# Keys and queries laid out features by rows, values by token, cum sent straight to rows, and product times in the planner: a fused attention and two-layer kernel

## Chip, cores and metric

One core of one Trainium2 chip. The metric is the device time of one execution in microseconds (us); three runs of the kernel before gave 899.12, 900.30 and 899.88, so a median of 899.88.

## What is computed

```python
def _attn_ref(q, k, v, f):               # 4 x 8 heads x 576 tokens x 64
    scores = scale * np.matmul(q, k.transpose(0, 1, 3, 2))
    cum = np.cumsum(np.log(np.clip(f, 0.0001, 1.0)), axis=-1)
    decay = cum[:, :, :, None] - cum[:, :, None, :]
    scores = np.where(causal, -1000000000.0, scores + decay)
    scores = scores - np.max(scores, axis=-1, keepdims=True)
    attn = np.exp(scores)
    attn = attn / (np.sum(attn, axis=-1, keepdims=True) + 1e-09)
    return np.matmul(attn, v)

def _moe_ref(x, w_in, w_out, g_ln):      # 2304 x 512, inner 1024
    h = x @ w_in
    e = np.exp(h - np.max(h, axis=-1, keepdims=True))
    solu = h * (e / (np.sum(e, axis=-1, keepdims=True) + 1e-09))
    mu, var = mean(solu), mean((solu - mu) ** 2)
    return ((solu - mu) / np.sqrt(var + 1e-06) * g_ln) @ w_out

def _moe2_ref(x, w_in, w_out):           # inner 2048
    h = np.maximum(x @ w_in, 0.0)
    return h * h @ w_out
```

The second layer takes the first's output, and the first takes the attention's. The weights come as 64-bit floats. Every large product is made of rounded single-precision parts: a number is split into a high part (rounded to the type of a fast product) and a low part (the rest), and three products (low x high, high x low, high x high) are added.

## The kernel before

The work is written as a list of steps. Each has the engines that it may run on with a duration that the planner assumes, a priority (a due time in ns), and what it reads and writes. `Plan.lay` simulates the engines with these durations: on each engine it takes, among the steps that could start first, the one of the smallest priority, and where a step may run on several engines, the one that is free first (VectorE only if it would end 650 ns sooner than the others). What comes out is the order of instructions on each engine (PE is TensorE, DVE VectorE, ACT ScalarE, POOL GpSimd); all DMAs stand in one order on SP's queue. On the chip the engines then run in that order and wait for each other by semaphores. So the assumed durations and the due times set the order, and nothing else.

**Attention** runs over 20 tiles of queries (five per sequence, four of 128 tokens and one of 64; the short one is last in sequences 0 and 2, first in 1 and 3), and in each tile over 8 heads. `load` (line 348) fetches keys, queries and values of a tile, 256 KB each in runs of 256 bytes, tokens by rows. `prep_k` (396) and `prep_q` (431) transpose them on TensorE, four products per tile and tensor (`transposed`, 366, line 372), into one of three PSUM buffers that other work uses as well. From there two copies make the high parts, two VectorE instructions (420 for keys, 443 for queries) the low parts, and `dup` (383, line 389) copies the high parts to the other 64 rows on GpSimd or by a DMA. A product has 128 rows: K1 and Q1 hold the high part on 64 rows and, on two of the others, the cumulated log decay (cum) in two parts against ones; K2 and Q2 hold low and high parts. So two products per head (479) give the scores with the decay of the keys. The masking and the row minimum run on VectorE (499), the exponential on ScalarE (513), the normalization on GpSimd (540), the transposes of the weights on TensorE (556) with a copy out of PSUM (278), and the products with the values on TensorE (577, `mix`).

**cum** is made at the start: f is loaded, clipped (1116), its logarithm taken (1119), summed by a scan over 576 columns (1127), split in two parts (1130, 1133), stored to DRAM (1104) and read back from there to the rows of K1 (412).

**First layer.** `weights1` converts its weights from 64 bits to a high and a low part (`convert`, 598: lines 618, 622, 626, 632, 636 and copies on 278 to 284). `first` (740) multiplies (761 to 763), takes the exponential and the layer norm, and `out1` (689) multiplies by the second weight (702 to 704), as soon as 128 tokens of attention are there.

**Second layer.** Its weights are converted (`weights2`) into the room that attention leaves, and `step` multiplies six blocks of 384 tokens (1033 to 1035, 1063 to 1065).

Due times come from `att_ns` (322, what a head should take on TensorE), `EACH` (the first layer's share), at least MINSLOT = 1150 ns per head, from T0 on.

## Time and profile before

| | us |
|---|---|
| median of three runs | 899.88 (899.12 to 900.30) |
| the profiled execution: its own time | 900.41 |
| its span, first to last instruction | 898.4 |
| TensorE busy in the span | 850.7 (95%) |
| VectorE, ScalarE, GpSimd busy | 504.8, 477.8, 322.9 |
| mean granted clock of TensorE, share of 2.4 GHz | 0.994 |
| moved by DMA | 65.27 MB in 99264 packets, 65440 under 512 bytes |

Busy time is a share of the span and says nothing of a stage. A table of stretches shows the same by stage. The chain of waits is followed back from the last instruction: a piece's time there is elapsed time, while the durations of TensorE's instructions overlap. In lists of waits the engine that waits stands first, then what it waited for.

### The profile page before, as it was taken

Reading aid. Unit: us, or ns where it says so; the run is one execution under the profiler, and the core shown is the slowest. Engines: PE = TensorE matmul, PEld = TensorE weight load, DVE = VectorE, ACT = ScalarE, POOL = GpSimd, SP = SyncE. Lnnn points to the kernel's source line nnn. Section 1 sums busy time; section 2 is a strip of 40 time slices with the busy share of each in tenths; the row PEclk is TensorE's granted clock in tenths of the full one; section 3 lists DMA queues with packets and bytes.
Section 4 is the critical chain, followed back from the end, with each engine's and each line's share of the span. In section 5 each row is a group of like instructions: output and inputs, shape, how many; then the busy total and the mean of one; then the engine's idle time right before and its main releaser. Section 6 shows DMA issues by size and latency. Waiting matters only on the chain.

```text
span 898.4 us, 15951 instructions
## 1 busy us (share of the span) xinstructions
PE 850.7 (95%) x5440; PEld 734.1 (82%) x5440; DVE 504.8 (56%) x1463; ACT 477.8 (53%) x1242; POOL 322.9 (36%) x503
## 2 busy tenths in 40 slices
PE   4898999999999999999989687999999999999998
PEld 3666788888888888888879676899899999999997
DVE  8998777765776667765599889222222222222221
ACT  6789766677666667765667666223322322322222
POOL 7988843333333344432588778100000000000000
PEclk9899999999999999999999999999999999999999
DMA  8644331122411224010546643005002002000000
GB/s 220 161 107 124 94 87 36 49 66 57 88 42 43 59 62 97 26 48 25 185 130 200 200 131 115 1 1 175 36 1 71 36 1 72 36 1 1 35 1 36
DMA packets 99345, 66.29 MB, mean 74 GB/s; under 512 B 65440, under 2 KB 89248, under 8 KB 99264
## 3 DMA queue, kind: packets, MB, share of 16 engines
q1 hardware_dynamic: 99264, 65.27, 25.6%
q8 instruction: 43, 0.70, 0.3%
q14 instruction: 38, 0.31, 0.1%
HBM read 49.51 MB, written 14.30 MB: 71 GB/s over the span
## 4 chain that ended last, share of the span: by engine, by line
PE 77%; DVE 12%; ACT 3%; issue 3%; POOL 3%; DMA 1%; SPq 0%; POOLq 0%; ACTq 0%; DVEq 0%
PE pp L1033 6%; PE pp L1034 6%; PE pp L1035 6%; PE z L479 6%; PE xo L577 6%; PE pp L556 6%; PE pp L702 3%; PE hp L761 3%; PE hp L762 3%; PE hp L763 3%; PE pp L703 3%; PE pp L704 3%; PE hp L1063 2%; PE hp L1064 2%; PE z L1065 2%
## 5 line engine op out<-in xcount | busy, mean ns | idle before, releaser
L1044 DVE CAST q<-q 128x384 fp32r<-128x384 f32 x96 | 40.5, 422 | 252.6 <-PE pp L1065 92.2
L1041 ACT ACTIVATE q<-pp 128x384 f32<-128x384 f32 x96 | 47.0, 490 | 232.5 <-PE pp L1035 230.5
L540 POOL TENSOR_SCALAR adj<-adj,st 128x128 f32<-128x128 f32 (+9 forms) x160 | 92.0, 577 | 172.7 <-DVE st L536 75.8
L513 ACT ACTIVATE adj<-z,st 64x288 f32<-64x288 f32 (+9 forms) x192 | 95.7, 501 | 33.9 <-DVE st L499 19.5
L479 PE MATMUL z<-k,q 128*128 128x256 f32 (+8 forms) x384 | 96.2, 344 | 6.2 <-ACT adj L513 6.0
L278 ACT COPY pt<-pp 128x256 f32<-128x256 f32 (+5 forms) x170 | 69.0, 423 | 46.3 <-PE pp L556 43.6
L702 PE MATMUL pp<-ln,woh 128*128 128x256 f32 x288 | 84.5, 293 | 0.4 <-POOL woh L282 0.4
L556 PE MATMUL pp<-ident,adj 128*128 128x128 f32 (+1 forms) x480 | 77.8, 275 | 6.0 <-POOL adj L540 2.6
L703 PE MATMUL pp<-ln,wol 128*128 128x256 f32 x288 | 81.2, 282 | 0.1
L499 DVE CUSTOM_DVE_ANT_0 z<-z,maskb 128x128 f32<-128x128 f32 (+8 forms) x144 | 65.9, 460 | 27.4 <-PE z L479 25.6
L704 PE MATMUL pp<-ln,woh 128*128 128x256 f32 x288 | 81.1, 281 | 0.0
L556 PEld LDWEIGHTS pp<-ident,adj 128*128 128x128 f32 (+1 forms) x480 | 53.1, 141 | 26.5 <-POOL adj L540 10.3
L479 PEld LDWEIGHTS z<-k,q 128*128 128x128 f32 (+1 forms) x384 | 57.5, 185 | 16.1 <-ACT adj L513 10.2
L577 PE MATMUL xo<-pt,vn 128*64 128x128 f32 (+1 forms) x960 | 68.1, 274 | 0.1
L577 PEld LDWEIGHTS xo<-pt,vn 128*64 128x64 f32 x960 | 49.5, 138 | 20.0 <-issue 13.5
L761 PE MATMUL hp<-wih,xl 128*128 128x512 f32 x144 | 61.8, 429 | 0.5 <-ACT hp L800 0.5
L763 PE MATMUL hp<-wih,xh 128*128 128x512 f32 x144 | 57.2, 397 | 0.0
L762 PE MATMUL hp<-wil,xh 128*128 128x512 f32 x144 | 57.1, 397 | 0.0
L702 PEld LDWEIGHTS pp<-ln,woh 128*128 128x128 f32 x288 | 54.4, 189 | 2.8 <-issue 1.0
L703 PEld LDWEIGHTS pp<-ln,wol 128*128 128x128 f32 x288 | 54.4, 189 | 0.7 <-DVE wol L636 0.3
L704 PEld LDWEIGHTS pp<-ln,woh 128*128 128x128 f32 x288 | 54.3, 189 | 0.0
L1043 ACT ACTIVATE q<-q 128x384 f32<-128x384 f32 x96 | 50.3, 524 | 2.4
(481 smaller groups left out, 2260.7 us busy)
## 6 DMA issues: line engine op xcount, KB each, us to landing
x2d<-xc SPq DMA_DIRECT2D x72, 128.0 KB
pt<-in_moe_w_in_dram SPq DMA_DIRECT2D x22, 256.0 KB
pt<-in_moe_w_out_dram SPq DMA_DIRECT2D x22, 256.0 KB
vn<-in_v_dram SPq DMA_DIRECT2D x20, 256.0 KB
ln<-x2d SPq DMA_DIRECT2D x24, 192.0 KB
out_dram<-pt SPq DMA_DIRECT2D x18, 256.0 KB
kn<-in_k_dram SPq DMA_DIRECT2D x16, 256.0 KB
qn<-in_q_dram SPq DMA_DIRECT2D x16, 256.0 KB
```

The source lines that it names most:

```text
L278: nc.scalar.copy(dst(), src())
L479: nc.tensor.matmul(dst, lhsT=ql[:, p, 0:m], rhs=rhs, start=(g == 0), stop=(g == 1))
L513: nc.scalar.activation(out=adj[0:m, c[1] : c[2]], in_=Z[c[0]][0:m, 0 : c[2] - c[1]], func=AF.Exp, bias=st[0:m, low : low + 1], scale=-1.0, ...
L540: nc.gpsimd.tensor_scalar(out=adj[0:m, 0:ext], in0=adj[0:m, 0:ext], scalar1=st[0:m, 5:6], scalar2=1.0, op0=ALU.mult, op1=ALU.mult,)
L556: nc.tensor.transpose(at(sk)[:, (c - g) * m : (c - g + 1) * m], adj[0:m, zc : zc + P], ident[0:m, 0:m])
L577: nc.tensor.matmul(XO[own[j], p, off : off + m], lhsT=VN[vslot[b, c]][:, (2 * p + j) * D : (2 * p + j + 1) * D], rhs=pts[j][:, c * m : (c ...
L702: nc.tensor.matmul(px, lhsT=woh[:, fc, w], rhs=lo, start=(fc == 0), stop=False)
L703: nc.tensor.matmul(px, lhsT=wol[:, fc, w], rhs=hi, start=False, stop=False)
L704: nc.tensor.matmul(px, lhsT=woh[:, fc, w], rhs=hi, start=False, stop=(fc == KF - 1))
L761: nc.tensor.matmul(HP[:, c], lhsT=XL[i][:, cc, :], rhs=wih[:, cc, w], start=(cc == 0), stop=False)
L762: nc.tensor.matmul(HP[:, c], lhsT=XH[i][:, cc, :], rhs=wil[:, cc, w], start=False, stop=False)
L763: nc.tensor.matmul(HP[:, c], lhsT=XH[i][:, cc, :], rhs=wih[:, cc, w], start=False, stop=(cc == KC - 1))
```

## The change

Keys and queries are laid out on the host: per tile and half of the heads (0 to 3, 4 to 7) the 64 features stand on 64 rows, and once more on the other 64, with heads and tokens along the row. So a tile is loaded in two DMAs per tensor (256 KB each for 128 tokens) in runs of 2 KB, and no transpose is needed. KN and QN hold the two halves of one tile, where they held two tiles. Values come by token with all heads in a row.

`prep_k` copies 128 rows (K1 then holds the high part twice) and makes the low part on VectorE or GpSimd from the loaded tile and K1; `prep_q` copies the high part twice (to Q2 and to the other rows of Q1) and makes the low part on VectorE. `dup` and `fill` are gone. cum stands on 16 rows of K2 (8 heads, two parts), the same for every head, and Q2 has ones on the two rows of its head (`picks`, from the identity). The second product of the scores has 80 rows. Heads are numbered by half: `j, p = divmod(h, 4)`.

At the start clip, logarithm and scan are cut into columns 0 to 127 and the rest; the parts of the first 128 columns go by DMA from SBUF to K2, and the way over DRAM serves the later tiles.

The planner's times for products are changed, with them the due times, and T0 is 10000 for 16000.

```diff
+    AUX = slice(D, D + 2 * H)
+    HH = H // 2
...
+    K1 = [new(f"k1{j}", [HH, KW], F32R) for j in range(2)]
+    K2 = [new(f"k2{j}", [HH, KW], F32R) for j in range(2)]
+    Q1 = [[new(f"q1{i}{j}", [HH, P], F32R) for j in range(2)] for i in range(2)]
+    Q2 = [[new(f"q2{i}{j}", [HH, P], F32R) for j in range(2)] for i in range(2)]
...
     def att_ns(T):
         t, m = T["t"], T["m"]
-        return 2 * max(107, T["ext"] / 2.4) + 53 + (t + 1) * m * (109 + 135) / 128 + 109
-    EACH = 24 * 216 + 48 * 109 + 872
+        return 2 * max(118, 0.4375 * T["ext"] + 6) + (t + 1) * 109 * (m / 128 + 1) + 130
+    EACH = 24 * 231 + 48 * 119 + 872
...
-    def load(n, prio):
+    def load(nm, dst, src, n, prio):
         T = tiles[n]
...
+        m, o = T["m"], HH * T["q0"]
+        for j in range(2):
+            pl.add(
+                dict(dma=800 * m / P),
+                lambda j=j: nc.sync.dma_start(dst[j][:, 0 : HH * m], src[T["b"], j, :, o : o + HH * m]), prio + 2 * j,
+                writes=[(nm, j)],
+            )
+    def load_k(n, prio):
+        load("kn", KN, k, n, prio)
+    def load_q(n, prio):
+        load("qn", QN, q, n, prio + 1)
+    def load_v(n, prio):
+        b, t = tiles[n]["b"], tiles[n]["t"]
+        vslot[b, t] = n % NV
         def fn():
...
+            nc.sync.dma_start(VN[n % NV], v[b, t * P : t * P + P])
+        pl.add(dict(dma=800), fn, max(prio + 4, V0), writes=[("vn", n % NV)])
+    def picks(i, j):
         def fn():
...
+            c = D + HH * j
+            a, b = (ident[AUX, x : x + HH].unsqueeze(2).broadcast_to([2 * H, HH, P]) for x in (c, c + H))
+            eng = nc.gpsimd if s.on == "pool" else nc.vector
+            eng.tensor_tensor(out=Q2[i][j][AUX], in0=a, in1=b, op=ALU.add)
+        s = pl.add(dict(dve=602, pool=1252), fn, -6.9e6 if i == 0 else 5000, ["ident"], [("qa", i, j)])
     def prep_k(n, prio):
         T = tiles[n]
         m, b, q0 = T["m"], T["b"], T["q0"]
         kc = kcol(b, T["t"])
         cs = slice(kc, kc + m)
-        fresh = b == 0 or (b == 1 and T["t"] < 2)
-        sk, tp = transposed(KN[n % 2], m, prio, [("kn", n % 2)])
+        los = {}
         for j in range(2):
...
+            raw = KN[j][:, 0 : HH * m].rearrange("p (h s) -> p h s", s=m)
+            hk, lk = kcells("kh", j, kc, kc + m), kcells("kl", j, kc, kc + m)
+            def lo(j=j, raw=raw):
+                eng = nc.gpsimd if los[j].on == "pool" else nc.vector
+                eng.tensor_tensor(out=K2[j][LO, :, cs], in0=raw[LO], in1=K1[j][LO, :, cs].bitcast(F32), op=ALU.subtract)
+            def auxrows(y, j=j):
+                if n:
+                    src = cumd[y, b, :, q0 : q0 + m]
+                else:
+                    src = XH[0][0:H, y, :].bitcast(F32)
+                dst = K2[j][D + y * H : D + y * H + H, :, cs].bitcast(F32)
+                nc.sync.dma_start(dst, src.unsqueeze(1).broadcast_to([H, HH, m]))
+            copy(HH * m, lambda j=j: K1[j][:, :, cs], lambda raw=raw: raw, prio + 2 * j, [("kn", j)], hk, psum=False)
+            los[j] = pl.add(
+                dict(dve=67 + 1.045 * HH * m, pool=119 + 2.213 * HH * m), lo, prio + 2 * j, [("kn", j)] + hk, lk
+            )
+            for y in range(2):
+                rk = [f"cumd{y}"] if n else [("c0", 0), ("xh", 0, 0)][y : y + 1]
+                pl.add(
+                    dict(dma=350), lambda y=y, auxrows=auxrows: auxrows(y), prio + 2 * j, rk,
+                    writes=kcells(f"ka{y}", j, kc, kc + m),
                 )
...
     def prep_q(n, prio):
         m = tiles[n]["m"]
         i = n % 2
-        q1, q2 = Q1[i], Q2[i]
-        sk, tp = transposed(QN[i], m, prio, [("qn", i)])
         for j in range(2):
...
+            q1, q2 = Q1[i][j], Q2[i][j]
+            raw = QN[j][:, 0 : HH * m].rearrange("p (h s) -> p h s", s=m)
+            for rows, dst, nm in ((LO, q2, "qh"), (HI, q1, "qd")):
+                copy(
+                    HH * m, lambda rows=rows, dst=dst: dst[rows, :, 0:m], lambda rows=rows, raw=raw: raw[rows],
+                    prio + 2 * j, [("qn", j)], [(nm, i, j)], (), SC, False,
+                )
+            def lo(q1=q1, q2=q2, raw=raw):
                 nc.vector.scalar_tensor_tensor(
-                    out=q2[j][other[j], :, 0:m], in0=tp()[own[j]], scalar=SC,
-                    in1=q1[j][own[j], :, 0:m].bitcast(F32), op0=ALU.mult, op1=ALU.subtract,
+                    out=q1[LO, :, 0:m], in0=raw[LO], scalar=SC, in1=q2[LO, :, 0:m].bitcast(F32), op0=ALU.mult,
+                    op1=ALU.subtract,
                 )
...
+            pl.add(dict(dve=67 + 1.045 * HH * m), lo, prio + 2 * j, [("qn", j), ("qh", i, j)], [("ql", i, j)])
...
-            for g, (ql, kr) in enumerate(((Q1[i][j], K1[j]), (Q2[i][j], K2[j]))):
-                rhs = kr[:, p, k0 + a : k0 + e]
+            for g, (ql, kr, r) in enumerate(((Q1[i][j], K1[j], P), (Q2[i][j], K2[j], AUX.stop))):
+                rhs = kr[0:r, p, k0 + a : k0 + e]
                 dst = z[0:m, 0 : rep * (e - a)]
                 if rep > 1:
-                    rhs = rhs.unsqueeze(1).broadcast_to([P, rep, ext])
+                    rhs = rhs.unsqueeze(1).broadcast_to([r, rep, ext])
                     dst = dst.rearrange("p (r x) -> p r x", x=ext)
...
+                nc.tensor.matmul(dst, lhsT=ql[0:r, p, 0:m], rhs=rhs, start=(g == 0), stop=(g == 1))
+        rk = [(c, i, j) for c in ("qh", "ql", "qd", "qa")]
+        for c in ("ka0", "ka1", "kh", "kl"):
             rk += kcells(c, j, k0, k0 + ext)
         for c, k_ in zip(cuts, zk):
-            mm = max(107, (c[2] - c[1]) / 2.4 + 2.5)
+            mm = 0.4375 * rep * (c[2] - c[1]) + 6
...
-        pl.add(dict(pe=(t + 1) * 270 * m / P), fn, prio, rk, ["xo"])
+        pl.add(dict(pe=(t + 1) * 218 * m / P + 200), fn, prio, rk, ["xo"])
...
-                pl.add(dict(pe=654), fn, prio, rk, [sk], take=sk if g == 0 else None, uses=[sk] if g else [])
+                pl.add(dict(pe=714), fn, prio, rk, [sk], take=sk if g == 0 else None, uses=[sk] if g else [])
...
-                    dict(pe=648), fn, a + d * FH * (c * KC + cc) / 8, xk + [("wi", cc, c, y) for y in "hl"], ["h"]
+                    dict(pe=693), fn, a + d * FH * (c * KC + cc) / 8, xk + [("wi", cc, c, y) for y in "hl"], ["h"]
...
-                dict(pe=6 * 162.5), up, prio, rk, [ck], take=ck if cc0 == 0 else None, uses=[ck] if cc0 else []
+                dict(pe=6 * 174), up, prio, rk, [ck], take=ck if cc0 == 0 else None, uses=[ck] if cc0 else []
...
+    load_k(0, -8e6)
+    load_q(0, -8e6)
+    load_v(0, -8e6)
+    ones = E[0 : B * H, P : P + S]
     pl.add(dict(dve=20), lambda: nc.vector.memset(mhalf, -0.5), -9.1e6, [], ["mhalf"])
+    pl.add(dict(pool=460), lambda: nc.gpsimd.memset(ones, 1.0), -9.1e6, [], ["ones"])
+    pl.add(dict(pool=700), lambda: make_identity(nc, ident), -8.9e6, [], ["ident"])
     pl.add(
         dict(act=1283 + 94), lambda: nc.scalar.activation(out=ST[1][:, 0:1], in_=mhalf, func=AF.Ln, scale=-1.0), -9.1e6,
         ["mhalf"], [("st", 1, 0)],
     )
...
+    c0 = [XH[0][0 : B * H, a, :] for a in range(2)]
+    for y, (a, e) in enumerate(((0, P), (P, S))):
+        w = slice(a, e)
+        n = e - a
+        def scan(w=w, a=a):
+            nc.vector.tensor_tensor_scan(
+                out=cu[:, w], data0=ones[:, w], data1=lf[:, w], initial=cu[:, a - 1 : a] if a else 0.0, op0=ALU.mult,
+                op1=ALU.add,
+            )
+        pl.add(
+            dict(dve=68 + 0.522 * n),
+            lambda w=w: nc.vector.tensor_scalar(
+                out=fl[:, w], in0=fl[:, w], scalar1=1e-4, scalar2=1.0, op0=ALU.max, op1=ALU.min
+            ), -9e6 + y, ["f"], [("f", y)],
+        )
+        pl.add(
+            dict(act=94 + 0.833 * n), lambda w=w: nc.scalar.activation(out=lf[:, w], in_=fl[:, w], func=AF.Ln),
+            -9e6 + y, [("f", y)], [("lf", y)],
+        )
+        pl.add(
+            dict(dve=200 + 2 * n), scan, -9e6 + y, [("lf", y), "ones"] + ["cu0", ("xh", 0, 0)] * y, [f"cu{y}"]
+        )
+        if y == 0:
+            pl.add(dict(dve=135), lambda: nc.vector.tensor_copy(c0[0], cu[:, 0:P]), -9e6, ["cu0"], [("c0", 0)])
+            pl.add(
+                dict(dve=201),
+                lambda: nc.vector.tensor_tensor(out=c0[1], in0=cu[:, 0:P], in1=c0[0].bitcast(F32), op=ALU.subtract),
+                -9e6, ["cu0", ("c0", 0)], [("xh", 0, 0), ("xh", 0, 64)],
+            )
     pl.add(
         dict(act=1283 + 94), lambda: nc.scalar.activation(out=ST[0][:, 0:1], in_=mhalf, func=AF.Exp), -9e6,
-        ["mhalf", ("adj", 1, 0), ("adj", 1, 1)], [("st", 0, 0)],
+        ["mhalf", ("lf", 0), ("lf", 1)], [("st", 0, 0)],
     )
-    pl.add(dict(dve=607), lambda: nc.vector.memset(fl, 1.0), -9e6, [], [("adj", 0, 0), ("adj", 0, 1)])
+    pl.add(dict(act=573), lambda: nc.scalar.copy(part(0), cu), -6e6, ["cu0", "cu1"], pt0[0])
...
             if h == PK and n + 1 < NQ:
                 prep_k(n + 1, when[s])
+                if n + 2 < NQ:
+                    load_k(n + 2, when[s])
             if h == PQ and n + 1 < NQ:
                 prep_q(n + 1, when[s])
+                if n + 2 < NQ:
+                    load_q(n + 2, when[s])
...
-DUPK0, DUPQ0, DUPK1 = 20, 20, 4
 V0, LOAD1 = -15000.0, 3000.0
-T0 = 16000.0
+T0 = 10000.0
...
         if name == "v":
             b, h, s, d = a.shape
...
+            pad = _np.zeros((b, s + 64, h * d), a.dtype)
+            a = a.transpose(0, 2, 1, 3).reshape(b, s, h * d)
+            pad[0::2, 0:s] = a[0::2]
+            pad[1::2, 0:64] = a[1::2, 0:64]
+            pad[1::2, 128:] = a[1::2, 64:]
             a = pad
+        if name in "qk":
+            b, h, s, d = a.shape
+            a = a.reshape(b, 2, h // 2, s, d).transpose(0, 1, 4, 2, 3)
+            lay = _np.empty((b, 2, 2, d, h // 2 * s), a.dtype)
+            for i in range(b):
+                cuts = list(range(0, s, 128)) + [s] if i % 2 == 0 else [0] + list(range(s % 128, s + 1, 128))
+                for x, y in zip(cuts, cuts[1:]):
+                    lay[i, :, :, :, h // 2 * x : h // 2 * y] = a[i, :, None, :, :, x:y].reshape(2, 1, d, -1)
+            a = lay.reshape(b, 2, 2 * d, h // 2 * s)
```

## Rows read from the trace of the kernel before

**Rows 1.** Stretches of the span: us, busy us (instructions) by engine, granted clock, DMA.
```profile
0.00:13.00 13.00, 4.12 (x17) 2.98 (x17) 9.88 (x16) 8.10 (x13) 8.93 (x24) 1.00 0.75 170
13.00:60.00 47.00, 38.19 (x202) 27.10 (x200) 42.34 (x132) 36.04 (x102) 40.14 (x54) 0.93 0.65 169
60.00:100.00 40.00, 36.10 (x260) 26.73 (x262) 35.72 (x109) 34.68 (x92) 34.88 (x55) 1.00 0.44 117
100.00:430.00 330.00, 329.31 (x2666) 279.72 (x2668) 228.14 (x833) 220.08 (x627) 130.75 (x226) 1.00 0.22 57
430.00:560.00 130.00, 109.81 (x636) 96.28 (x633) 112.10 (x211) 86.67 (x230) 102.50 (x139) 0.99 0.53 164
560.00:898.40 338.40, 333.20 (x1670) 301.28 (x1668) 76.64 (x164) 92.20 (x181) 5.70 (x8) 1.00 0.10 33
```
Columns by engine: TensorE products, TensorE weight loads, VectorE, ScalarE, GpSimd; then granted clock, DMA share, GB/s.

**Rows 2.** The same view, two stretches of the start.
```profile
15.00:35.00 20.00, 14.28 (x56) 9.31 (x56) 19.62 (x64) 14.87 (x47) 17.51 (x23) 1.00 0.87 234
35.00:42.00 7.00, 6.42 (x26) 5.28 (x27) 5.14 (x17) 4.51 (x13) 6.84 (x8) 0.51 0.40 111
```

**Rows 3.** Waits from 100 to 430 us: total us, times, longest.
```profile
POOL adj L540 <- DVE st L536: 73.3, 38, 6.1
ACT pt L278 <- PE pp L556: 37.3, 51, 2.9
```

**Rows 4.** Stretches for line 372 alone: products, weight loads, clock, DMA.
```profile
60.00:100.00 40.00, 1.17 (x12) 0.90 (x12) 1.00 0.44 117
100.00:430.00 330.00, 16.48 (x112) 12.29 (x112) 1.00 0.22 57
```

**Rows 5.** Chain of waits, 290 to 400 us: start, us, what.
```profile
293.27 0.39 PE pp L372 x4
...
323.24 0.44 PE pp L372 x4
```

**Rows 6.** Line 372's instructions: shortest, median, longest in ns, first and last start.
```profile
L372 PE MATMUL pp<-ident,kn x80: 222/273/473, 4.8 to 376.5; 128*128 128x128 f32 x64, 64*128 64x64 f32 x16
...
L372 PE MATMUL pp<-ident,qn x80: 222/272/476, 5.9 to 393.6; 128*128 128x128 f32 x64, 64*128 64x64 f32 x16
```

**Rows 7.** Timeline, 0 to 13 us: start, us, engine, line, what.
```profile
2.76 0.56 DVE L1116 TENSOR_SCALAR adj<-adj 32x576 f32<-32x576 f32 x1 [0.71 <-DMA adj<-in_f_dram]
...
3.36 0.68 ACT L1119 ACTIVATE adj<-adj 32x576 f32<-32x576 f32 x1 [1.14 <-DVE adj L1116]
...
4.78 1.09 PE L372 MATMUL pp<-ident,kn 128*128 128x128 f32 x4 [4.78 <-DMA kn<-in_k_dram]
...
5.24 1.34 DVE L1127 TENSOR_TENSOR_SCAN adj<-adj,adj 32x576 f32<-32x576 f32 x1
...
5.87 1.11 PE L372 MATMUL pp<-ident,qn 128*128 128x128 f32 x4
...
7.55 1.38 SPq L1104 DMA_DIRECT2D cumd<-pt  x2
...
10.42 0.57 SPq L412 DMA_DIRECT2D k<-cumd  x2
...
12.94 0.56 PE L479 MATMUL z<-k,q 128*128 128x256 f32 x1
```

**Rows 8.** Groups by line, 0 to 100 us: a ScalarE copy from SBUF.
```profile
L278 ACT CAST wih<-ln 128x512 fp32r<-128x512 f32 x8 | 4.9, 615 | 1.5 <-POOL ln L632 1.3
```

**Rows 9.** VectorE lines with two inputs: shortest, median, longest in ns.
```profile
L420 DVE TENSOR_TENSOR k<-pp,k x40: 410/683/695, 7.0 to 379.4; 64x512 fp32r<-64x512 f32 x32, 64x256 fp32r<-64x256 f32 x8
...
L626 DVE SCALAR_TENSOR_TENSOR ln<-ln x8: 691/732/1666, 11.2 to 46.8; 128x512 uint32<-128x512 uint32 x8
...
L1047 DVE TENSOR_TENSOR kn<-q,q x48: 547/559/1103, 453.6 to 824.2; 128x384 fp32r<-128x384 f32 x48
```

**Rows 10.** GpSimd's duplications, line 389.
```profile
L389 POOL TENSOR_SCALAR k<-k x36: 401/616/1070, 6.7 to 378.7; 64x512 fp32r<-64x512 f32 x32, 64x256 fp32r<-64x256 f32 x4
```

127 lines of the change are left out of this document (21 added, 106 removed).

## Prediction

> **What bounds the kernel now.** I read the table of stretches first, because the page's shares are averages over stages with different limits [rows 1]. The reader is to see three kinds of stage. From 100 to 430 us TensorE is busy for 329.31 of 330 us at full clock while VectorE has 228 and GpSimd 131: TensorE is the bound. From 560 us to the end it is so again (333.20 of 338.40). Between 430 and 560 us VectorE is busy for 112.10 of 130 and TensorE idles for 20.19; that is the conversion of the second layer's weights. The first 100 us are the third kind: TensorE idles for 8.88 us until 13, for 8.81 from 13 to 60 and for 3.90 from 60 to 100. Together 21.6 of the 47.7 us idle in the span lie there.
>
> The second view cuts the start finer [rows 2]. Between 15 and 35 us VectorE is busy for 19.62 of 20 us, TensorE for 14.28: weight conversion, softmax and the preparation of keys share VectorE. Between 35 and 42 us the granted clock is 0.51, the 1.2 GHz level, after a stretch in which TensorE waited; it is the only long piece at that level.
>
> The waits of 100 to 430 us show which engine the others wait for [rows 3]: ScalarE's copy out of PSUM waits 37.3 us for transposes of TensorE, and GpSimd stands idle 73.3 us for a reciprocal. Only one of these could end on TensorE's path, since TensorE itself has next to no idle time there.
>
> **Transposes removed.** The change takes out all of L372: 160 instructions, four per group, two groups per tile. By stretch, 112 lie in the TensorE-bound part, 12 from 60 to 100 us, the other 36 earlier [rows 4]. What one group is worth is read from the chain, not from the instructions' durations: a group of 128 tokens holds the chain for 0.44 us, a group of 64 for 0.39 [rows 5]. Of the 28 groups from 100 to 430 us four are of 64 tokens (tiles 14 and 15), so 24 x 0.44 + 4 x 0.39 = 12.1 us. The three groups from 60 to 100 us are of 64 tokens: 1.2 us, since TensorE is 90% busy there. The 36 earlier ones count nothing; TensorE waits there, and if that cover were gone they'd be worth 9 x 0.44 = 4.0 us. Upper bound of the main term: the union of their busy time, 16.48 us [rows 4]. The median instruction lasts 272 or 273 ns [rows 6], but successive ones overlap, so that isn't elapsed time.
>
> The Trainium skill ("TensorE: Matmul & The Clock Gate", Part 4: PE-mode transpose) gives about 275 ns for a 128x128 transpose inside a kernel. The instruction's duration agrees with it [rows 6]; taken as the price it would make 112 x 0.275 = 30.8 us of the main term where the chain says 12.1.
>
> **Start.** Today the first product of scores runs at 12.94 us [rows 7]. Its last input is the cumulated log decay: f is there at 2.76, clipping (0.56), logarithm (0.68), a scan over 576 columns (1.34), two splits, two stores to DRAM at 7.55 and the reload issued at 10.42. The change works the first 128 columns alone and sends them straight from SBUF to the rows of K2. By parts, from these rows: 2.76, clip 0.3, logarithm 0.3, scan 0.4, the two splits 0.5, hand-overs 0.4, issue 0.3, and landing 2.5 as the reload of today takes (10.42 to 12.94): 7.5 us. The other input, keys and queries: today the transposes of the first two 256 KB loads begin at 4.78 and 5.87, 1.09 us apart [rows 7]. Keys and queries now have twice the bytes, in four loads; the first of each is enough for heads 0 to 3. A copy from SBUF takes 0.615 us on ScalarE [rows 8], two for the queries, and the low part about 0.73 [rows 9], so 5.87 + 1.23 + 0.73 = 7.8 us. I take 7.5: 5.4 us earlier. At worst only the store and reload go (10.42 - 7.55 = 2.9); at best 6.5 us is reached (6.4).
>
> The loads: per tile 1.28 MB instead of 0.77. If bytes set the time, two more loads of 1.09 us; over four tiles 8.7 us of transfer in 60, beside 0.75 and 0.65 of busy DMA [rows 1], which still fits. If their longer runs (2 KB for 256 B) count, nothing. I take nothing. KN and QN now have one buffer per half instead of one per tile in turn, so the load for tile n + 2 waits on SP until the preparation of n + 1 has read them; behind it on SP stand weight pieces and cum rows. It has a whole tile of time, at least 8 x 1150 ns by the due times; I cost it at nothing, and at up to 2 us in the first 60. Per tile SP issues two more loads and two more cum-row DMAs: 4 x 0.3 to 0.4 us, on a queue that nobody waits for in the long stage.
>
> **Preparation work, 13 to 60 us.** Per tile GpSimd loses four duplications of about 0.6 us [rows 10]; ScalarE and VectorE read SBUF instead of PSUM and make six copies instead of four; four low parts stay, of which the two for keys may go to GpSimd. The zero and one fills go, four picks come. What VectorE gains depends on the planner: if the keys' low parts go to GpSimd, 4 tiles x 2 x 0.69 = 5.5 us; if they stay, nothing. I take 2.
>
> Against it stands a property of the new low parts. L420 reads one operand from PSUM: its 40 instructions never exceed 695 ns, however busy GpSimd is. L626 and L1047 read both from SBUF: medians 732 and 559, maxima 1666 and 1103 [rows 9]. So a low part from SBUF is 0.05 us longer at rest and up to 0.97 when GpSimd runs. Sixteen in the first four tiles: 0.8 to 15.5 us of VectorE in a stretch where it is full. The Trainium skill ("SBUF — State Buffer", Who interferes with whom) says that a VectorE instruction with two SBUF inputs, or a one-input copy in a two-port mode, contends with GpSimd for one shared port, and that the second to issue waits for the other's whole instruction; the trace agrees (L626's 1666 against 691). By it the start would lose what it gains; the rival below prices that from rows.
>
> **Planner.** The new product times (693 for 648, 1044 for 975 and so on) and the first due time (10 for 16 us) change no instruction, only the order on each engine. Worked out from the diff's constants the due times end at 396.6 us instead of 394.7, so weights, first layer and attention keep their relative order except at the start. I count 0, and plus or minus 5 us, since the 20.19 us of idle time from 430 to 560 hang on order.
>
> **Sum.** 12.1 + 1.2 + 5.4 + 2.0 = 20.7 us. The profiled execution, span 898.4, would have 877.7; with the 1.5 us by which the median of the runs (899.88) lies above that span, 879.2 us.
>
> **Rivals.** *The start gives it back.* The low parts and copies from SBUF block GpSimd and VectorE in the full stretch, about 0.5 us for each of sixteen, 8 us, so of the start's 7.4 nothing is left: gain 13 us, 887. For: 19.62 of 20 us [rows 2], L626's maximum. Against: ten operations per tile instead of twelve.
>
> *Transposes were cover.* TensorE's busy share is modelled; if a chain of VectorE and GpSimd is close behind, their time becomes idle time. Only half is then gained, and the start whole: 20.7 - 6.6 = 14.1, and less order, 892 at the worst. Against: [rows 3], where the others wait for TensorE.
>
> *More than that.* Three PSUM buffers are no longer held for copy and split of keys and queries, and better product times fill half of the 20.19 us: 10 us more, 869.
>
> *Slower.* The shared access decides the long stage. From 100 to 430 us there are some 15 tiles with four low parts, 60, each able to hold or be held by up to 0.97 us: 58 us. GpSimd's normalization stands in each head's chain just before TensorE's transpose of the weights. With half of it on that path, 29 us more against 20.7 less: 908. It turns the sign when more than a third (20.7 of 58) gets through. Against: GpSimd has 199 us free there, VectorE 102 [rows 1].
>
> *It doesn't do what it says*: the scores still wait for a slow start, for instance since the four loads of the first tile land late. The start's 7.4 us are lost and nothing else: 887, as the first rival.
>
> **How the numbers follow.** Forecast 0.60; start given back (either way) 0.16; cover 0.07; more 0.11; slower 0.06. The predicted time is the forecast's, 879.2. Its own bounds: the start at 2.9 instead of 5.4 and no relief, 884; the start at 6.4, relief 5.5 and the union 16.48, 870. For 8 in 10 I reach from half of the third rival to the first rival and most of the second: 868 to 890. A measurement of this kernel can tell about 0.2% from no change, so faster means below 898.1. Faster 0.91, same 0.03, slower 0.06.
>
> **What the new profile should show.** No transposes of keys and queries, and TensorE still over 98% busy in the middle, which ends some 12 us sooner by its own length. The first product of scores at 7 to 8 us; if it is at 10 or later, the start is wrong. The low parts with a maximum well over 0.7 us; if that maximum comes often before 60 us and the first layer (line 761) starts no sooner, the first rival holds. TensorE waiting for GpSimd's normalization in the middle would be the slow case. The stage of weight conversion should keep its 130 us; if it shrinks or grows by more than 5, the planner's order did more than I allow.

## The result, and the profile after

The changed kernel takes 912.75 us (median of 911.96 to 913.91), the kernel before 900.09 in the same measurement: the ratio is 1.0143, 95% interval 1.0127 to 1.0159. It is slower by 12.7 us where 20.7 us less were forecast. The profiled execution has a span of 910.1 us against 898.4.

The same stretches as in [rows 1], with the same columns, of the kernel after:

```profile
0.00:13.00 13.00, 1.53 (x4) 1.00 (x4) 10.73 (x17) 6.64 (x11) 10.53 (x22) 1.00 0.63 194
13.00:60.00 47.00, 34.89 (x145) 22.41 (x145) 44.76 (x120) 32.58 (x92) 38.91 (x44) 0.93 0.63 193
60.00:100.00 40.00, 32.98 (x211) 23.73 (x209) 34.09 (x103) 30.82 (x76) 35.75 (x54) 0.83 0.37 112
100.00:430.00 330.00, 322.56 (x2563) 268.69 (x2563) 227.27 (x821) 221.66 (x633) 153.38 (x237) 1.00 0.26 79
430.00:560.00 130.00, 106.78 (x631) 92.29 (x628) 115.06 (x228) 89.55 (x237) 103.57 (x137) 0.97 0.54 168
560.00:910.10 350.10, 346.46 (x1735) 313.22 (x1734) 80.44 (x171) 94.46 (x185) 5.79 (x8) 1.00 0.10 32
```

The reader is to see that TensorE idles more in every stretch up to 560 us. From 100 to 430 us it stood still for 0.69 us, and now for 7.44; from 60 to 100 us it is busy for 3.12 us less, and that at a granted clock of 0.83 instead of 1.00. A fixed stretch doesn't hold the same work in both kernels, though. So I measure from two milestones of the work itself: the first product of scores of tile 5 (the first tile of the second sequence), and the last product of scores. For the kernel before and the kernel after, from the timelines (start, us, engine, line, what) and the lists of the score line (shortest, median, longest in ns, first and last start):

```profile
119.43 0.40 PE L479 MATMUL z<-k,q 128*64 128x256 f32 x2
130.30 0.70 PE L465 MATMUL z<-k,q 128*64 128x256 f32 x4
```
```profile
L479 PE MATMUL z<-k,q x384: 252/336/583, 12.9 to 428.8; 128*128 128x256 f32 x32, 128*64 128x288 f32 x32, 128*128 128x288 f32 x32, 128*128 128x384 f32 x16
L465 PE MATMUL z<-k,q x384: 252/329/797, 6.9 to 435.5; 128*128 128x256 f32 x32, 128*64 128x288 f32 x32, 128*128 128x288 f32 x32, 128*128 128x384 f32 x16
```

That splits the 11.7 us between the spans. The **first part**, to tile 5, is 10.9 us longer (130.3 against 119.4). The **long part**, from there to the last scores, is 4.2 us shorter (305.2 against 309.4). The **last part** is 5.0 us longer (474.6 against 469.6). It holds the conversion of the second layer's weights. TensorE is busy there for 447.7 us instead of 444.2 and idles for 26.9 instead of 25.4; two more triples of the first layer's products (line 747 is left 13 times, its counterpart 761 before 11 times) stand after the last scores. So the milestones don't hold exactly the same work of the layers either.

**The first part.** The timeline of the start (start, us, engine, line, what, idle before and releaser):

```profile
2.78 1.14 DVE L1118 TENSOR_SCALAR adj<-adj 32x128 f32<-32x128 f32 x2 [0.26 <-DMA adj<-in_f_dram]
3.94 0.68 DVE L383 TENSOR_TENSOR q<-ident 16x512 fp32r<-16x512 f32 x1
4.68 0.68 DVE L399 TENSOR_TENSOR k<-kn,k 64x512 fp32r<-64x512 f32 x1
5.29 0.50 DVE L1111 TENSOR_TENSOR_SCAN adj<-e,adj 32x128 f32<-32x128 f32 x1
...
6.91 0.55 PE L465 MATMUL z<-k,q 128*128 128x256 f32 x1 [6.91 <-DVE xh L1130]
...
6.93 0.99 DVE L383 TENSOR_TENSOR q<-ident 16x512 fp32r<-16x512 f32 x1
7.95 0.58 DVE L1133 TENSOR_TENSOR xh<-adj,xh 32x128 fp32r<-32x128 f32 x1
...
10.71 0.98 PE L465 MATMUL z<-k,q 80*128 80x256 f32 x3 [3.25 <-DMA k<-xh]
...
15.13 1.45 PE L465 MATMUL z<-k,q 128*128 128x256 f32 x3 [3.44 <-ACT adj L499]
```

The first product runs at 6.91 us, even before the 7.5 of the prediction. But a head has two products, and the second, with the rows of cum, waits until 10.71: line 383 (the rows that pick cum) and line 399 stand on VectorE ahead of the scan, and the four DMAs of cum take until then. The next scores come at 15.13. Of 6.0 us at the first product, 2.0 are left at the start of tile 1 (25.8 against 27.8), and tiles 3 and 4 are 1.6 and 9.6 us late (64.9 and 96.3 against 63.3 and 86.7).

The milestones of the tiles split it further. From the first product to tile 3 the changed kernel takes 58.0 us (before 50.4), for tile 3 31.4 (23.4), for tile 4 34.0 (32.7): 7.6, 8.0 and 1.3 us lost, less the 6.0 of the start. Stretches with the columns as above: tile 2 and tile 3 of the kernel after, then tile 3 of the kernel before:

```profile
43.20:64.90 21.70, 17.25 (x89) 10.18 (x89) 21.64 (x51) 15.99 (x41) 18.68 (x23) 0.84 0.32 96
64.90:96.30 31.40, 25.59 (x140) 18.17 (x141) 27.31 (x85) 23.85 (x59) 27.40 (x41) 0.78 0.37 112
63.30:86.70 23.40, 20.57 (x149) 15.24 (x148) 20.68 (x64) 20.65 (x54) 19.59 (x32) 1.00 0.49 125
```

In tile 2 VectorE is full (21.64 of 21.70 us). In tile 3 no engine is: VectorE 27.31 and GpSimd 27.40 of 31.40, TensorE 25.59 at a clock of 0.78. The plan put nine pieces of the conversion of the first layer's weights there (line 612), the kernel before six (line 626). What sets the pace of tile 3 no run shows.

Over the whole stretch from 16 to 96 us VectorE is busy for 74.03 of 80 us, TensorE for 63.08 (before: 72.81 and 69.53). VectorE's own rows of the preparation, 13 to 100 us, lines 433 and 399 of after and their counterparts 443 and 420 of before (shortest, median, longest):

```profile
L433 DVE SCALAR_TENSOR_TENSOR q<-qn,q x10: 419/904/2068, 16.0 to 92.2; 64x512 fp32r<-64x512 f32 x6, 64x256 fp32r<-64x256 f32 x4
L399 DVE TENSOR_TENSOR k<-kn,k x7: 634/711/1678, 17.0 to 73.7; 64x512 fp32r<-64x512 f32 x5, 64x256 fp32r<-64x256 f32 x2
L443 DVE SCALAR_TENSOR_TENSOR q<-pp,q x10: 419/684/694, 16.2 to 87.2; 64x512 fp32r<-64x512 f32 x6, 64x256 fp32r<-64x256 f32 x4
L420 DVE TENSOR_TENSOR k<-pp,k x9: 410/676/695, 14.7 to 82.0; 64x512 fp32r<-64x512 f32 x5, 64x256 fp32r<-64x256 f32 x4
```

The low parts of the queries sum to 10.05 us instead of 5.83, and the planner, which takes a copy from SBUF on VectorE for 0.335 us, put eight copies of keys and queries there (lines 287 and 289, two before) that last 5.5. With the low parts of the keys, 6.1, VectorE spends 21.7 us on keys and queries in this stretch, 12.1 before. The Trainium skill ("SBUF — State Buffer", Who interferes with whom) says that a VectorE instruction with two SBUF inputs shares a port with a GpSimd instruction that reads SBUF, and that the second to issue waits for the other. These rows agree: 694 at most with one input from PSUM, 2068 with both from SBUF.

Pieces at the half clock, 1.2 GHz, begin at 48.2, 68.7 and 85.8 us. The last, which begins as a wait of 2.78 us for an exponential ends (the columns of the stretches):

```profile
85.80:96.00 10.20, 8.94 (x34) 5.66 (x35) 7.68 (x32) 6.69 (x19) 8.78 (x14) 0.50 0.31 91
```

**The long part.** What TensorE waits for, 100 to 430 us, kernel after, the two largest (us in total, times, longest); before, all waits there together were 0.4 us:

```profile
PE pp L542 <- POOL adj L526: 3.8, 11, 0.8
PE z L465 <- ACT adj L499: 2.3, 5, 0.7
```

The transposes left, and in their place stand waits for GpSimd's normalization and ScalarE's exponential.

### The profile page after: what moved, and what is told of

The parts are those of the page before. It is cut to its first block, busy times and chain, and to the rows that moved or that the text cites. A ratio compares the mean times of both kernels' runs of the same rounds, so it can differ in the third digit from the quotient of the medians.

```text
span 910.1 us, 15615 instructions
## 1 busy us (share of the span) xinstructions
PE 845.2 (93%) x5280; PEld 721.3 (79%) x5280; DVE 512.4 (56%) x1455; ACT 475.7 (52%) x1232; POOL 347.9 (38%) x497
## 2 busy tenths in 40 slices
DMA packets 55503, 75.29 MB, mean 83 GB/s; under 512 B 7456, under 2 KB 35104, under 8 KB 55424
## 4 chain that ended last, share of the span: by engine, by line
PE 68%; DVE 14%; POOL 6%; issue 4%; ACT 4%; DMA 3%; SPq 0%; POOLq 0%; ACTq 0%; DVEq 0%
PE pp L1019 6%; PE pp L1021 6%; PE pp L1020 6%; PE pp L542 5%; PE z L465 5%; PE xo L563 4%; PE hp L747 3%; PE hp L749 3%; PE hp L748 3%; PE hp L1049 2%; PE hp L1050 2%; PE hp L1051 2%; PE pp L688 2%; PE z L1051 2%; PE z L1050 2%
## 5 line engine op out<-in xcount | busy, mean ns | idle before, releaser
L526 POOL TENSOR_SCALAR adj<-adj,st 128x128 f32<-128x128 f32 (+9 forms) x160 | 98.1, 617 | 145.0 <-DVE st L522 98.5
L465 PE MATMUL z<-k,q 128*128 128x256 f32 (+17 forms) x384 | 96.7, 351 | 25.5 <-ACT adj L499 15.0
L281 ACT COPY pt<-pp 128x256 f32<-128x256 f32 (+5 forms) x174 | 71.0, 426 | 41.4 <-PE pp L542 39.8
L542 PE MATMUL pp<-ident,adj 128*128 128x128 f32 (+1 forms) x480 | 79.8, 281 | 12.3 <-POOL adj L526 11.0
L465 PEld LDWEIGHTS z<-k,q 128*128 128x128 f32 (+3 forms) x384 | 59.5, 190 | 39.2 <-ACT adj L499 20.3
L563 PE MATMUL xo<-pt,vn 128*64 128x128 f32 (+1 forms) x960 | 70.0, 280 | 0.0
L747 PE MATMUL hp<-wih,xl 128*128 128x512 f32 x144 | 63.7, 442 | 0.9 <-ACT hp L786 0.7
L1029 ACT ACTIVATE q<-q 128x384 f32<-128x384 f32 x96 | 50.4, 525 | 2.7
```

Source lines behind the costliest of these rows:

```text
L281: nc.scalar.copy(dst(), src())
L465: nc.tensor.matmul(dst, lhsT=ql[0:r, p, 0:m], rhs=rhs, start=(g == 0), stop=(g == 1))
L526: nc.gpsimd.tensor_scalar(out=adj[0:m, 0:ext], in0=adj[0:m, 0:ext], scalar1=st[0:m, 5:6], scalar2=1.0, op0=ALU.mult, op1=ALU.mult,)
L542: nc.tensor.transpose(at(sk)[:, (c - g) * m : (c - g + 1) * m], adj[0:m, zc : zc + P], ident[0:m, 0:m])
L563: nc.tensor.matmul(XO[own[j], p, off : off + m], lhsT=VN[vslot[b, c]][:, (2 * p + j) * D : (2 * p + j + 1) * D], rhs=pts[j][:, c * m : (c ...
L747: nc.tensor.matmul(HP[:, c], lhsT=XL[i][:, cc, :], rhs=wih[:, cc, w], start=(cc == 0), stop=False)
```

## The experiments

Milestones of all kernels, from their timelines as above: start of tile 5, from there to the last scores, from there to the end of the span, us.

| kernel | to tile 5 | long part | last part | median of runs |
|---|---|---|---|---|
| before | 119.4 | 309.4 | 469.6 | 900.09 |
| after | 130.3 | 305.2 | 474.6 | 912.75 |
| layout, old times | 133.5 | 302.8 | 469.8 | 907.1 |
| the same, T0 = 10000 | 132.1 | 302.7 | 469.5 | 905.5 |
| after, T0 = 16000 | 132.6 | 304.1 | 474.8 | 914.9 |
| old layout, new times | 128.5 | 313.0 | 477.6 | 922.6 |
| old layout, attention times | 117.5 | 309.6 | 470.6 | 899.7 |
| old layout, layers' times | 122.4 | 312.2 | 471.6 | 908.6 |
| old layout, SLACK 40 | 123.4 | 310.2 | 474.0 | 909.7 |
| old layout, MINSLOT 1200 | 128.8 | 310.4 | 469.7 | 909.7 |
| before, transposes cut | 118.2 | 304.7 | 470.1 | 894.7 |
| after, first products x5 | 132.0 | 303.5 | 474.9 | 914.0 |
| after, first products x10 | 142.4 | 304.5 | 474.2 | 923.8 |
| after, low part of Q x4 | 143.0 | 304.0 | 475.7 | 924.2 |
| after, searched | 126.4 | 296.6 | 480.9 | 906.0 |
| layout, old times, searched | 126.2 | 300.8 | 469.9 | 899.1 |
| layout, VectorE times, not searched | 127.4 | 306.6 | 470.2 | 906.1 |
| layout, VectorE times, searched | 125.8 | 293.8 | 473.5 | 895.1 |
| layout, attention times, searched | 126.2 | 296.0 | 470.8 | 895.3 |
| old layout, attention times, searched | 122.3 | 309.5 | 471.4 | 903.6 |

### Which part of the change

Four kernels take the change apart: the layout with the times and due times of before; the times alone on the old layout; the changed kernel with T0 of before; and with the old times but its own T0. Shown is a part of the first one's edit, against the kernel after.

```diff
-        return 2 * max(118, 0.4375 * T["ext"] + 6) + (t + 1) * 109 * (m / 128 + 1) + 130
+        return 2 * max(107, T["ext"] / 2.4) + 53 + (t + 1) * m * (109 + 135) / 128 + 109
...
-                pl.add(dict(pe=714), ...
+                pl.add(dict(pe=654), ...
...
-T0 = 10000.0
+T0 = 16000.0
```

> The new layout and start of cum with the product times, due times and T0 of before (16000). Three theories for the 12.7 us by which the changed kernel is slower than before (912.75 against 900.09). Work: the operations that the new layout gives VectorE and GpSimd cost the time; then this stays at 905 to 918. Order: the new product times and the due times from them cost it; then this falls to what the removed transposes and the earlier start promised, 876 to 890. Due: T0 at 10000 alone costs it; then this is 876 to 895 as well.

> The kernel before with the new product times and the due times from them, T0 left at 16000 and layout untouched. Work: within 3 us of before, 897 to 903. Order: slower than before by most of the 33 us that are missing against the forecast, 912 to 930. Due: within 3 us of before.

> The changed kernel with T0 back at 16000. Due (weights of the first layer stand behind attention in the order, so TensorE lacks first-layer products before 100 us and its clock falls): 880 to 897, and the stretch 60 to 100 us at a granted clock of 1.00. Order and work: within 5 us of the changed kernel, 908 to 918.

> The changed kernel with the product times and due-time formulas of before, T0 at 10000. Order: 876 to 890. Due: as the changed kernel, 905 to 918. Work: as the changed kernel, 905 to 918. If this and the run with T0 back at 16000 both recover a part, the two act through the same order of weights and attention.

Measured: 907.1 us (ratio 1.0089, 1.0074 to 1.0104), 922.6 (1.0263, 1.0246 to 1.0280), 914.9 (1.0171, 1.0147 to 1.0196) and 905.5 (1.0062, 1.0045 to 1.0079). The first due time, T0, is not it. The times alone, with the due times that follow from them, touch no instruction and cost 23 us; on the new layout they cost 7 to 8. And the layout without them still loses 6 to 8 us, though 160 instructions of TensorE are gone. So none of the three theories holds alone: order is right for the second kernel, work for the first and the last. In all four tile 5 starts 9 to 14 us late.

### Is a new plan by itself a loss, and what is a transpose worth

Two kernels change one constant of the planner in the kernel before and no instruction. One keeps its plan and issues one transpose of a group's four, from the first groups on (111 of 160 are left out; stale values take their place in the scores). One is the 905.5 us kernel with constants searched for the shortest plan of its own planner.

```diff
-SLACK = 20
+SLACK = 40
```
```diff
-MINSLOT = 1150
+MINSLOT = 1200
```
```diff
+    whole = {}
...
-            for p in range(NP):
+            some = 1 if whole.get(pl.slot[sk]) else NP
+            whole[pl.slot[sk]] = 1 if m == P else whole.get(pl.slot[sk])
+            for p in range(some):
```

> The kernel before with one constant of the planner changed (a step may be chosen up to 40 ns later than the earliest instead of 20), so that it plans anew; not one instruction is added, removed or changed in size. Theory Tuned (the constants of the kernel before were fitted to its own costs, and any new plan with the same constants loses by its order): 5 to 15 us more, 904 to 914 us. Theory Neutral (a new plan is as good as the old one, and what was lost in the changed kernel was lost by its operations): within 3 us of the kernel before, 896 to 902 us.

> The kernel before with another constant of the planner changed (the least time between the due times of two heads 1200 instead of 1150 ns): a second plan anew of the same instructions. Theory Tuned: 5 to 15 us more, 904 to 914 us. Theory Neutral: within 3 us, 896 to 902 us.

> The kernel before with its plan, constants, costs and order of instructions unchanged, but from the first groups on only one of the four transposes of a group is issued (so three quarters of the keys and queries of the later tiles are stale; their scores are wrong, the work on them is the same). It removes about 110 transposes. Theory Worth (the transposes were TensorE time that the end feels, as the prediction had it): three quarters of its 13.3 us, so 10 us less, about 889 us. Theory Cover (they ran in time in which TensorE would have waited for the exponentials and the normalization anyway): 0 to 3 us less, 897 to 900 us. If Worth holds, the order of the re-planned kernels lost the gain; if Cover holds, there was little to gain.

> The changed kernel with the old product times (the kernel that took 905.5 us) and nine constants of the planner searched anew for it: SLACK 80, T0 6000, MINSLOT 1100, POUT0 40000, LAG 10, V0 -5000, TAILR 1.4, W2P 6000, S1D 14000. Theory Tuned: constants fitted to the new costs win back about 10 us, 890 to 898 us, faster than the kernel before. Theory Neutral with slower preparation (the operations on VectorE and GpSimd from SBUF are what costs): constants don't help, 903 to 908 us.

Measured: both neutral plans 909.65 us (1.0108, 1.0092 to 1.0123; 1.0110, 1.0095 to 1.0125). So the same instructions in another order lose 10 us, in the first part (4 to 9 us) and, in one, in the last. With the old order the cut transposes give 5.0 us (894.66; 0.9941, 0.9924 to 0.9957), half of the 10 that the prediction's price makes of them, and 4.7 of it in the long part. Stretches of the kernel with cut transposes, as above, and then the long part of three kernels, by the milestones: before, with cut transposes, after:

```profile
60.00:100.00 40.00, 36.52 (x270) 26.99 (x271) 34.71 (x106) 34.84 (x92) 34.66 (x57) 1.00 0.46 122
100.00:430.00 330.00, 327.92 (x2620) 275.62 (x2620) 230.45 (x838) 222.65 (x636) 130.71 (x228) 1.00 0.23 59
```
```profile
119.40:428.80 309.40, 309.25 (x2488) 263.77 (x2487) 214.13 (x786) 206.54 (x587) 118.53 (x207) 1.00 0.22 57
118.20:422.90 304.70, 303.47 (x2408) 255.94 (x2407) 213.90 (x786) 205.86 (x587) 117.84 (x207) 1.00 0.23 57
130.30:435.50 305.20, 299.74 (x2375) 251.16 (x2374) 204.72 (x765) 203.44 (x580) 130.05 (x205) 1.00 0.25 78
```

The long part of the kernel before has 108 transposes, this one has 27. By the prediction's price the 81 left out are 8.8 us. TensorE's busy time fell by 5.8 us, its idle time rose from 0.15 to 1.23 us, and 4.7 us came back. So most of what is missing, 3.0 us, was never there to be had: an instruction left out took 0.07 us off the busy time, where the price says 0.11. Only 1.1 us turned into idle time, and none of the waits in its list is for the normalization or the exponential. In the changed kernel the busy time fell by 9.5 us, but 5.3 us of it came back as idle time, and there the waits are for those two.

With the order held the first part keeps its clock too: the drop at 60 to 100 us does not come from the missing transposes.

The searched constants give 899.1 us, 6.4 less than unsearched. That lies between the two theories (890 to 898 and 903 to 908) and leaves the layout level with the kernel before (0.9991, 0.9981 to 1.0000).

### What sets the pace of the first part

In the changed kernel, in its own order, either TensorE or VectorE gets more work in tiles 1 to 3 (the run with ten products has 9 for the 4 of the first diff).

```diff
+                for _ in range(4 if g == 0 and 1 <= n <= 3 else 0):
+                    nc.tensor.matmul(dst, lhsT=ql[0:r, p, 0:m], rhs=rhs, start=True, stop=True)
```
```diff
+                for _ in range(4 if 1 <= n <= 3 else 1):
                     nc.vector.scalar_tensor_tensor(
                         out=q1[LO, :, 0:m], ...
```

> The changed kernel in its own order, with the first product of each head of tiles 1 to 3 (25.8 to 96 us) issued five times instead of once, the repeats overwritten: the same result, some 96 products of 0.12 to 0.23 us, 16.7 us more for TensorE at full clock. Theory TensorE (the stretch up to 100 us is set by TensorE's time): 12 to 17 us more, 925 to 930 us. Theory Clock (TensorE has gaps there, and what hurts is the half clock that follows them): the repeats fall into the gaps, the granted clock of 60 to 100 us rises from 0.83 to above 0.95, and the end comes 3 to 6 us earlier, 907 to 910 us. Theory VectorE (VectorE and GpSimd, 9 tenths busy there, set the pace): the clock may rise, the end stays within 4 us, 909 to 917 us.

> The changed kernel with the first product of each head of tiles 1 to 3 issued ten times: some 216 products, 37.6 us more for TensorE at full clock than in the changed kernel, against 16.7 us in the run that cost 1.2 us. Theory VectorE (TensorE has some 20 us of gaps and 7 us of half clock there): the gaps are used up and 10 to 20 us show, 923 to 933 us, at a granted clock of 1.00 in 60 to 100 us. Theory Free (TensorE's time does not matter there at all): under 5 us more, below 918 us.

> The changed kernel in its own order, with VectorE's low part of the queries of tiles 1 to 3 computed four times instead of once (the repeats write the same values): 18 more operations of about 0.74 us, 13.3 us more for VectorE before 96 us, nothing more for TensorE. The mirror of the run with 16.7 us more for TensorE there, which cost 1.2 us. Theory VectorE (VectorE sets the pace up to 100 us): 9 to 14 us more, 922 to 927 us. Theory Chain (neither engine alone, but the order in which they wait for each other): 3 to 7 us more, 916 to 920 us. Theory Slack (VectorE has room too): within 2 us.

Measured against 912.75: 16.7 us more for TensorE give 913.95 (1.2 more, not clear of noise), 37.6 give 923.83 (11.1 more), and the four low parts give 924.15 (11.4 more). The doses of TensorE are the estimates on record. The dose of VectorE, 13.3 us by its estimate, is 15.0 us by the trace: 24 low parts sum to 22.2 us where the changed kernel's six take 7.2. Stretches of the run with five products, of the run with ten, then of the one with four low parts:

```profile
60.00:100.00 40.00, 35.48 (x245) 27.25 (x245) 33.41 (x101) 30.85 (x76) 34.07 (x53) 1.00 0.33 106
```
```profile
13.00:60.00 47.00, 39.85 (x243) 33.33 (x244) 41.06 (x111) 29.36 (x83) 35.56 (x41) 1.00 0.59 183
60.00:100.00 40.00, 39.93 (x247) 33.12 (x246) 28.00 (x88) 25.34 (x65) 25.18 (x41) 1.00 0.29 91
```
```profile
13.00:60.00 47.00, 29.28 (x114) 19.05 (x114) 44.42 (x111) 27.16 (x77) 31.05 (x36) 0.88 0.58 181
60.00:100.00 40.00, 31.07 (x174) 22.37 (x172) 38.68 (x101) 27.99 (x69) 29.74 (x44) 0.80 0.33 94
```

Most of VectorE's time counts (tile 3 comes 12.9 and tile 5 12.7 us later for 15.0 us); the first 16.7 us of TensorE's are almost free, and only the larger dose, which fills TensorE (39.93 of 40 us) and empties VectorE (28.00), shows. The clock theory is not borne out by the smaller dose: the granted clock from 60 to 100 us rose from 0.83 to 1.00 (the span's mean from 0.984 to 0.990), and the end came no sooner, where 3 to 6 us were to come back.

These doses reach less far than "up to 100 us". All 24 low parts run from 16.0 to 70.7 us, before tile 3 starts in that run (77.8), and tile 3 itself then takes 30.3 us, not more than the 31.4 of the changed kernel. So VectorE's work sets the pace up to tile 3; for the 8.0 us lost in tile 3 that is not shown. Nor was a dose given to GpSimd, which is as busy in tile 3 as VectorE, or to ScalarE.

### Which of the new times

> The kernel before with only the new times of the attention products in its planner (scores, mixes, and the due times that follow from them); the times of the layers' products stay old. All new times together took 922.6 us on this layout, other new plans without new times 909.7 us. Theory Any plan (it is the planning anew alone): 907 to 913 us. Theory Attention times (these are what spoils the order): 917 to 923 us.

> The kernel before with only the new times of the layers' products in its planner (EACH, 714, 693 and 6 x 174 ns); the attention's stay old. Theory Any plan: 907 to 913 us. Theory Layer times (longer planned products put the layers' products after the weights' conversion differently, so that TensorE waits longer at 430 to 560 us): 917 to 923 us.

```diff
-EACH = 24 * 216 + 48 * 109 + 872
+EACH = 24 * 231 + 48 * 119 + 872
...
-dict(pe=654)
+dict(pe=714)
...
-dict(pe=648)
+dict(pe=693)
...
-dict(pe=6 * 162.5)
+dict(pe=6 * 174)
...
-dict(pe=648)
+dict(pe=693)
```

On the old layout the attention's times alone take 899.7 us (0.9996, 0.9987 to 1.0006), the layers' times alone, shown here, 908.6 (1.0104, 1.0089 to 1.0119). Neither explains the 922.6 of both: they don't add. The first is also the one new plan of the old layout that costs nothing (it reaches tile 5 even 1.9 us sooner, at 117.5), so a new plan does not always lose.

### Is the layout worth anything once the constants fit

Constants were searched for four more plans: the changed kernel with all new times; the layout with old product times but measured times for the preparation on VectorE and GpSimd; the layout with the attention's new times only; and the old layout with the attention's new times. The second also ran with its constants unsearched. Its costs (the added term `dve` is 0.54 * HH * m for the copies of keys and queries):

```diff
-        s = pl.add(dict(dve=602, pool=1252), fn, ...
+        s = pl.add(dict(pool=1262), fn, ...
...
+            ns["dve"] += dve
...
-dict(dve=67 + 1.045 * HH * m, pool=119 + 2.213 * HH * m)
+dict(dve=67 + 1.2 * HH * m, pool=139 + 2.23 * HH * m)
...
-dict(dve=67 + 1.045 * HH * m), lo, prio + 2 * j, [("qn", j), ...
+dict(dve=67 + 1.31 * HH * m), lo, prio + 2 * j, [("qn", j), ...
```

> The changed kernel with its new product times, and the planner's constants searched anew for it: LAG 11, S0 11500, PIN0 14000, FH 0.35, FO 0.5, PQ 7, V0 3000, MINSLOT 1050. The same search brought the layout with old times from 905.5 to 899.1 us. Theory Tuned: 6 to 10 us less than the changed kernel, 903 to 907 us. Theory Times (measured times make a better plan once the constants fit): 890 to 898 us, under the retuned layout with the old times.

> The new layout with the old product times, where the planner has measured times for the new operations on VectorE and GpSimd instead (the copy of a 512 row from SBUF 612 ns on VectorE instead of 335, the low parts of K 684 and of Q 736 instead of 602, of K on GpSimd 1280), the rows that pick cum made on GpSimd alone, and the constants searched anew (LAG 12, DOWN 9500, FH 0.2, FO 0.8, P2 2000, POUT 2500, POUT0 45000, SLACK 10, V0 -5000). Theory VectorE (true costs of what binds the first 100 us are what the plan lacks): 885 to 895 us. Theory Draw (any searched plan of this layout comes to the same): 896 to 903 us.

> The new layout with the new times of the attention products and the old times of the layers' products, constants searched anew (PIN 4500, V0 -5000, FO 0.8, SHIFT 600, P2 -4000, TAILR 1.2, LAG 10, PQ 4, S0 11500, PK 3, POUT 3000, PIN0 14000, S1D 14000, T0 6000). On the old layout the attention's times alone cost nothing (899.7 us) and the layers' times 8.7 us. Theory Layer times (they are what hurts, on this layout too): 893 to 900 us, under the 906.0 us of the search with all new times. Theory Draw: 900 to 907 us.

> The kernel of 895.1 us (new layout, old product times, measured times of the preparation on VectorE and GpSimd, pick rows on GpSimd) with the planner's constants of the changed kernel, not searched. With the old preparation times this plan took 905.5 us. Theory Costs (true preparation times are what the plan lacked): 895 to 899 us. Theory Search (the fitted constants brought it): 902 to 908 us.

> The old layout with the new attention times (899.7 us unsearched) and the constants searched for it as for the new layout (W2P 5500, FO 0.6, FH 0.3, TAILR 1.2, SLACK 60, P2 0). Theory Layout (only the layout without transposes reaches 895 us): 897 to 905 us. Theory Search (any searched plan does, the layout is worth nothing): 893 to 896 us.

Measured, in this order: 905.98 us (1.0070, 1.0055 to 1.0085), 895.07 (0.9956, 0.9940 to 0.9971), 895.31 (0.9956, 0.9940 to 0.9971), 906.1 (1.0072, 1.0057 to 1.0087) and 903.55 (1.0042, 1.0025 to 1.0059). The truer preparation times alone brought nothing (906.1 against 905.5); the constants did, 11 us. But a search is no sure gain: it looks for the shortest plan by the planner's own durations, and on the old layout with the attention's times it made the kernel 3.9 us slower (903.55 against 899.70 unsearched). So the old layout did not get there by the same search, but that is one draw and does not show that it can't. Two versions of the layout thus beat both kernels, the kernel before by 4 us. Stretches and score line of the one with the attention's times:

```profile
60.00:100.00 40.00, 34.12 (x213) 25.17 (x213) 32.60 (x96) 29.84 (x72) 35.37 (x54) 0.83 0.36 107
100.00:430.00 330.00, 325.96 (x2630) 275.55 (x2630) 233.28 (x847) 222.50 (x641) 158.38 (x245) 1.00 0.28 84
430.00:560.00 130.00, 113.40 (x608) 98.55 (x607) 113.88 (x210) 86.32 (x226) 108.38 (x143) 0.97 0.51 158
```
```profile
L465 PE MATMUL z<-k,q x384: 251/330/792, 6.9 to 422.2; 128*128 128x256 f32 x32, 128*64 128x288 f32 x32, 128*128 128x288 f32 x32, 128*128 128x384 f32 x16
```

Its first part is still 6.8 us longer than before (126.2 against 119.4), at a clock of 0.83 from 60 to 100 us. It wins 13.4 us in the long part and gives 1.2 back in the last.

## Why the prediction was wrong

**Transposes, 12.1 us in the long stretch.** The mechanism was right, the size wrong. In the changed kernel the long part is 4.2 us shorter, with the layout and old times 6.6 and 6.7. Two steps failed. The first is the price: the 0.44 us that a group holds in the chain, 0.11 an instruction, was taken for the time that goes with it. With the order held an instruction left out took 0.07 us off TensorE's busy time, which makes some 8 us of the 112 instructions instead of 12.1. The second is the reading of [rows 1] as a bound without a second: TensorE 329.31 of 330 us busy says that nothing else ends later now, not by how much. With the order held 1.1 of 5.8 us turned into idle time, in the changed kernel's own order 5.3 of 9.5, as waits for the normalization and the exponential.

The rival *transposes were cover* said that half would be gained. At the held order half it was, but mainly because the price was too high; in the changed kernel its mechanism is seen. I gave it 0.07, because [rows 3] showed others waiting for TensorE. Those waits show who is late now, not the distance to the next bound. With searched constants the layout's long part shrinks by 8.6 to 15.6 us, of which the last part gives back 0.3 to 11.3. From tile 5 to the end TensorE is then busy for 745.0 to 748.8 us, before for 753.5: so 4.7 to 8.5 us of its time were to be had, but not with this plan.

**The 1.2 us from 60 to 100 us.** Not there: TensorE is not the bound in that stretch of the changed kernel, as 16.7 us of extra products show, and with the transposes cut at the held order tile 3 takes 23.4 us as before (62.1 to 85.5).

**Start, 5.4 us.** The first product came 6.0 us sooner, and the step holds only as far as it goes. I followed one input of the first product and not the second product, the cum rows' DMAs behind it and what stands on VectorE. And the 6.0 us at the first product are 2.0 at tile 1. The working itself has a slip of 0.3 us: of 7.5 for cum and 7.8 for keys and queries it took the earlier, where the later one counts.

**Preparation relief, 2.0 us.** Wrong in sign: VectorE's time for keys and queries from 13 to 100 us rose from 12.1 to 21.7 us. The rival *the start gives it back* named the right mechanism, low parts from SBUF that are held up, and the right row. It priced them at 8 us and let them cancel the start's 7.4 at most, when the 0.8 to 15.5 us stood in the text; and it put no price on the copies that the planner moves to VectorE. Of the 9.6 us more, 7.5 stand before tile 3. With the rate of the run with four low parts, 12.9 us for 15.0, they would cost 6.5 of the 7.6 us that are lost up to there. That is worked out, not shown: two neutral plans of the old layout lose 4.0 and 9.4 us in the first part without it, and the order and the added work were not separated there. The 8.0 us of tile 3 it does not explain: only 2.5 us of this work were added there. What runs with 15.2 to 21.2 us of this work and searched constants have in common is a first part of 126 us.

**Planner, 0 plus or minus 5 us.** As far as the runs show, this step decided the sign: the same layout takes 895.1 to 914.9 us by its planner's times and constants alone. I compared due times and took it that a plan with nearly equal due times is nearly the same plan; T0 itself, put back, changed the time by 2.1 us. A changed cost or constant sends the planner down another path: on the old layout new plans with unsearched constants gave -0.3, 9, 10, 10 and 23 us. The changed kernel's last part is 5.0 us longer, where the layout with old times has 469.8 and 469.5, as before.

**The slower rival** gave 908, near the result, for another reason: it put the loss in the long part, where the median of the normalization did rise from 538 to 588 ns and its maximum from 755 to 1377, but that part became shorter. That its number came close is luck.

**What was right**: no transposes, the first product before 8 us, maxima of the low parts far above 0.7 us. Of the signs that I named for a wrong prediction three came: TensorE under 98% in the middle (97.7), waits for the normalization there (3.8 us), and a first layer that starts no sooner (its first reduction at 58.6 us, 54.0 before).

Open stays why the order of the kernel before is so good up to tile 5, where every other plan in the table but one (the old layout with the attention's times) loses 3 to 14 us; what sets the pace of tile 3, where 8.0 us are lost; and why the two sets of new times add up to more than their sum.
